# A delta-rule scan with a feed-forward block: writing the first four units' outputs together, one feature of w_out at a time

## The chip, the cores and the metric

The kernel runs on one core of a Trainium2 chip. The core has a matrix engine (TensorE, PE in the profile), a vector engine (DVE), an activation engine (ScalarE, ACT), a general engine (GpSimd, POOL), a sync engine (SP) that mostly issues transfers, and 16 DMA engines. Matrix products end in PSUM, which the kernel divides into eight banks of 128 partitions by 2 KB. The metric is the device time of one execution in microseconds (us), lower is better.

## The reference

A linear-attention scan by the delta rule, followed by a feed-forward block. For 4 batches, 8 heads, 768 positions and a head size of 48:

```python
k_n = k / (norm(k) + 1e-6)
state = 0                                   # (B, H, 48, 48)
for t in range(768):
    y[:, :, t] = einsum('bhd,bhde->bhe', q[:, :, t], state)
    v_old      = einsum('bhde,bhd->bhe', state, k_n[:, :, t])
    state     += beta_t * outer(k_n[:, :, t], v[:, :, t] - v_old)
x = y as (3072, 384)                        # heads side by side
h = x @ w_in                                # (384, 2048)
g = h * sigmoid(1.702 * h)
out = g @ w_out                             # (2048, 384)
```

q, k, v and beta are float32. w_in and w_out arrive as float64: two 32-bit words a number, which the kernel itself turns into float32.

## The kernel before

**Units.** The 768 positions are cut into 6 chunks of 128. A chunk of one batch is a unit, so there are 24, taken chunk by chunk: units 0 to 3 are the four batches of chunk 0. Two units make a half, whose 256 rows go through the feed-forward block together.

**The scan.** Inside a chunk the delta rule becomes a triangular system. Its 32x32 diagonal blocks are inverted on DVE (`invert`, two units at once from chunk 1 on, one step of the generator being a product and a reduction); the blocks of G go to DRAM and back to be laid out for it (Nd, NT), as does the result (Yd, XB). A unit is then solved in four blocks of 32 rows: `solve` (psU) multiplies by the inverse, ACT copies to US, `below` (psR) computes what the later rows lose, DVE subtracts it from V. `scores` makes psT, QS and psQ with the mask M (POOL selects the triangle). `queries` and `outputs` make psY, two tiles of a bank each, hold the new state in a part of one of them (psS), copy the unit's y to xT and add psS to the state ST. `woven` interleaves the steps of up to three units and, by `spend`, pieces of the feed-forward queue; its tuple STEPS says how many steps of the inversion stand at each of three places for odd and even n.

**The feed-forward block.** `hidden` computes ph = x @ w_in for two features of 128 at a time and writes gT = gelu(ph). `written` sums po = g @ w_out over 16 features for one unit. For the first half `both_written` (L771) does this for two units feature by feature, in the list `order` of features, since w_out is still being converted then; the second half follows with `written`. The queue is set up at L1108.

**Conversion.** Raw float64 words of w_out are fetched by `fetch_out` (L188) into buffers that are free at that time: parts of w_out itself (`inside`) or turns of the xT and M buffers (`outside`). The first eight of the order go by the queue of GpSimd, the others by that of SP. `conversions` yields the five DVE operations of a piece one after the other, with a Relu on ACT after the first of them; `fill(n)` takes n of these steps. When a piece is done, `fetches` starts the fetch that may use its place.

**Order.** The operations of each engine run in the order in which the program records them in this part (`pinned`, `sync`, `other_queue`, `beside`); each engine works down its own list, and waits where an operand isn't ready or a buffer is in use.

**PSUM.** Two banks are `ps_big` (psT, psG, half of psQ), four are `ps_seq` (psU, psR, psY, the other half of psQ), two are `ps_moe` (ph, po). A tile takes the next bank of its pool in turn and waits for the last reader of what was there.

Of the kernel before, what the change touches and what calls it, by code (L numbers as in the profile page):

```python
# [18 lines left out]
def kernel(  # L19
# [23 lines left out]
    C = 128  # L43
# [23 lines left out]
    io = ctx.enter_context(tc.tile_pool(name="io", bufs=3))  # L67
    wk = ctx.enter_context(tc.tile_pool(name="wk", bufs=2))
    ps_big = ctx.enter_context(tc.tile_pool(name="ps_big", bufs=2, space=PSUM))
    ps_seq = ctx.enter_context(tc.tile_pool(name="ps_seq", bufs=4, space=PSUM))  # L70
    ps_moe = ctx.enter_context(tc.tile_pool(name="ps_moe", bufs=2, space=PSUM))
    dram = ctx.enter_context(tc.tile_pool(name="dram", bufs=2, space=bass.MemoryType.DRAM))

# [26 lines left out]
    def pinned(op):  # L100

        return lambda *a, **kw: tc.keep_in_program_order(op(*a, **kw))  # L102

    class Engine:

# [75 lines left out]
                )  # L181

    places, slots = {}, {}
    inside = {3: 6, 4: 8, 5: 10, 6: 12, 7: 14, 12: 14, 13: 10}
    outside = {0: "xT", 8: "xT", 11: "xT", 1: "M", 9: "M", 14: "M", 2: "M2", 10: "M2", 15: "M2"}
    order = [0, 1, 2, 3, 4, 5, 6, 7, 8, 13, 9, 10, 12, 11, 14, 15]

    def fetch_out(f):  # L188

        if f in outside:  # L190
            slot = outside[f]
            if slot not in slots:
                slots[slot] = wk.tile([128, 2 * DM], I32, tag=slot[:2].strip("2"), name="raw", bufs=3)
            words = slots[slot]
        else:
            words = raws[:, inside[f] * DM : (inside[f] + 2) * DM]
        places[f] = as_raw(words, (1, DM))
        first = order.index(f) < FC // 2
        (other_queue if first else sync)(
            out=as_rows(places[f])[:, 0], in_=moe_w_out[f * 128 : (f + 1) * 128, :]  # L200
        )

# [50 lines left out]
    def conversions():  # L253

        whole = list(pieces())

        def begin(i):
            dst, raw, shape, name = whole[i]
            ops = conversion(dst, places[name[1]] if raw is None else raw, shape)
            next(ops)  # L260
            return ops

        after = begin(0)
        yield
        for i in range(len(whole)):
            ops = after
            next(ops)
            yield
            next(ops)
            yield  # L270
            if i + 1 < len(whole):
                after = begin(i + 1)
                yield
            next(ops)
            yield
            next(ops)
            done.add(whole[i][3])
            fetches.pop(whole[i][3], lambda: None)()
            yield
# [1 line left out]
    fetches = {  # L281
        ("in", 0, 1): lambda: fetch_in(3),
        ("in", 3, 1): lambda: fetch_out(3),
        ("out", 4): lambda: fetch_out(13),
        ("out", 6): lambda: fetch_out(12),
    }
    for new, old in ((8, 0), (9, 1), (10, 2), (11, 8), (14, 9), (15, 10)):
        fetches[("out", old)] = lambda f=new: fetch_out(f)
    converting = conversions()

# [266 lines left out]


    def bank(name, shape=(128, H, D)):
        return ps_seq.tile(list(shape), F32, tag="seq", name=name)  # L560

    lasts = [None]

    class Step:
# [19 lines left out]
        def scores(self):  # L584
# [7 lines left out]
            if c > 0:  # L592
# [1 line left out]
                act.activation(self.QS[:, :, S], St, ACT.Copy)  # L594
            yield
            self.M = (
                spare("M").rearrange("p (h t) -> p h t", h=H) if self.n in (B - 1, B + 1)
                else wk.tile([128, H, 128], F32, tag="M", name="M", bufs=3)
            )
            n = 128 + D if c > 0 else 128  # L600
            for g in range(0, NP, 2):
                pool_, tag = (ps_seq, "seq") if g else (ps_big, "big")
                ps = [pool_.tile([128, 2, 128 + D], F32, tag=tag, name="psQ") for _ in range(2)]
                for i in range(2):
                    for hh in range(2):
                        r = self.rows(hh)
                        pe.matmul(
                            ps[hh][:, i, 0:n], lhsT=self.kT[r, g + i, :],
                            rhs=self.QS[r, g + i, 0:n], start=True, stop=True,
                        )  # L610
                for hh in range(2):
                    hs = slice(2 * g + hh, 2 * g + 4, 2)
                    if c > 0:
                        Vh = self.V[:, hs, :]
                        vec.tensor_tensor(Vh, Vh, ps[hh][:, :, S], op=ALU.subtract)
                    copy = act.copy if hh == 0 or self.n < 2 * B + HB else vec.tensor_copy
                    copy(self.M[:, hs, :], ps[hh][:, :, 0:128])
                if g == 0:
                    yield
# [148 lines left out]
            nc.sync.dma_start(out=out[b * S + c * C : b * S + (c + 1) * C, :], in_=o)  # L768
            yield 1.3

    def both_written(c, gT):  # L771

        po = [ps_moe.tile([128, DM], F32, tag="moe", name="po") for _ in range(HB)]
        for n, f in enumerate(order):
            ahead = order[min(n + 3, FC - 1)]
            while ("out", ahead - ahead % 2 if 4 <= ahead < 8 else ahead) not in done:
                fill(1)
            for i in range(HB):
                pe.matmul(
                    po[i], lhsT=gT[f // FQ][:, f % FQ, i * C : (i + 1) * C], rhs=w_out[:, f, :],  # L780
                    start=(n == 0), stop=(n == FC - 1),
                )
            if n < FC - 1:
                yield 1.3
        for i in range(HB):
            o = wk.tile([128, DM], F32, tag="o", name="o")
            act.copy(o, po[i])
            sync(out=out[i * S + c * C : i * S + (c + 1) * C, :], in_=o)
        yield 1.3

    def take(cost):
# [73 lines left out]
            debt[0] -= done  # L865

    STEPS = (9, 5, 3, 3, 3, 3)
    begun = {}

    def woven(n, share):  # L870

# [3 lines left out]
        nonlocal inverting  # L875
        A, B_, D_ = steps.pop(n - 1, None), steps.get(n), steps.get(n + 1) or NoStep()
        m = n + B + 1
        if n < B + HB:
            K = normalize_mixed(m + 1) if n <= B else iter(())
        else:  # L880
            K = (normalize if n > 6 else normalize_mixed)(m) if m < len(units) else iter(())
# [2 lines left out]
            P = begun.pop(m)  # L884
        if n % HB == 1 and B < n and n + 1 + HB < len(units):
            inverting = invert(*units[n + 1 + HB], HB)
        ahead = STEPS[:3] if n % HB == 1 else STEPS[3:]

        next(K, None)
        together([(B_, 1)], [(A, 2)])  # L890
        run(D_.scored)
        next(K, None)
# [10 lines left out]
        together([(B_, 2)], [(D_, 0)])  # L903
        if A:
            A.queries()
            A.outputs()
        run(P)
        ahead_of(inverting, ahead[2])
        if n % HB == 0:
            run(inverting)  # L910
        spend(share / 6)
# [41 lines left out]
    late_U = room[:, 0 : H * D + XR]  # L953
    pool.memset(late_U[:, H * D :], 0.0)
    zs = room[:, 512 : 512 + 6 * B * H].rearrange("p (s b h) -> p s b h", s=6, b=B)
    psD = [ps_seq.tile([128, B, NP, BS], F32, tag="seq", name="psD") for _ in range(2)]
    warm(NW)
    for b in range(B):
        squares_first(b)
# [133 lines left out]
    load(B + 2, ((QP, q),), sync)  # L1093
    for n in range(2 * B + 1, 2 * B + 1 + HB):
        load(n, ((KN, k),), sync)
    for i in range(22):
        ahead_of(inverting, 1)
        if i < 18:
            feed()
        if i in (2, 3, 4, 7, 8, 9, 10):  # L1100
            fetch_out(i - 2 if i < 5 else i - 3)
    run(inverting)
    def beside_conversion(work):
        for cost in work:
            fill(2)
            yield cost

    queue = [beside_conversion(w) for w in ffn] + [both_written(0, gTs[0]), written(*units[HB], gTs[1])]  # L1108
    for n in range(B - 1, len(units) + 1):
        woven(n, 20.8 if n > 6 else 13.0)  # L1110
    run(take(1e9))
# [31 lines left out]
```

## Time and profile before

| | us |
|---|---|
| median of 3 runs | 771.1 |
| lowest and highest | 770.93, 772.66 |
| the profiled execution | 771.55 |
| its span | 769.8 |
| PE busy | 743.6 |
| DVE busy | 439.8 |
| ACT busy | 240.1 |
| POOL busy | 128.4 |
| first po begins | 135.13 |
| first ph of the third half | 215.10 |

The profile is of one execution. The span runs from its first to its last instruction, and lies 1.75 us under the execution's own time. Busy time is counted by engine. A row such as `po<-w_out,gT` names the tile that is written and the tiles read; a bracket at the end of a row of the timeline gives the idle time before it and the operation that ended it. The granted clock is the share of full speed at which TensorE was allowed to run. All recorded operations of the scan have one line, L102, so that rows are told apart by their tiles.

### The profile page before, as it was taken

The numbers are of one execution on the slowest core, as the hardware profiler recorded it, in microseconds if no ns is written. First come the engines' busy times: TensorE is split into PE (matmuls) and PEld (weight loads), VectorE is DVE, ScalarE is ACT, GpSimd is POOL, SyncE is SP. The second block draws the span as 40 slices with busy tenths as digits, with TensorE's granted clock in tenths as the row PEclk, the third lists the DMA queues.
The fourth block names the chain that finished last, engine by engine and source line by source line (L and its number), as shares of the span: only waits on it lengthen the run. The fifth ranks groups of instructions, "written<-read, shape, count | busy, mean of one in ns | idle before, by whom it ended". The sixth has DMA issues, their size and how long they took to land.

```text
span 769.8 us, 19471 instructions
## 1 busy us (share of the span) xinstructions
PE 743.6 (97%) x8508; PEld 558.0 (72%) x8508; DVE 439.8 (57%) x896; ACT 240.1 (31%) x535; POOL 128.4 (17%) x133
## 2 busy tenths in 40 slices
PE   7888999888999999999999999999999999999997
PEld 6666788556687687687688678678678677686774
DVE  5999897996766566566566566565566521000000
ACT  4567523343233233133133133124123132121110
POOL 6133301100222122122131121220210000000000
PEclk8599999989999999999999999999999999999999
DMA  9965355543142142142142142142030020000000
GB/s 158 173 121 114 86 146 124 141 107 82 40 96 57 37 93 56 37 95 56 35 96 57 34 97 56 25 107 57 22 81 9 24 42 2 17 11 1 26 1 21
DMA packets 131637, 50.78 MB, mean 66 GB/s; under 512 B 106432, under 2 KB 127040, under 8 KB 131552
## 3 DMA queue, kind: packets, MB, share of 16 engines
q1 hardware_dynamic: 129152, 41.27, 24.9%
q0 software_dynamic: 2400, 8.26, 4.4%
q8 instruction: 67, 1.10, 0.6%
q14 instruction: 18, 0.15, 0.1%
HBM read 32.08 MB, written 16.25 MB: 63 GB/s over the span
## 4 chain that ended last, share of the span: by engine, by line
PE 83%; DVE 8%; SPq 4%; issue 1%; ACT 1%; DMA 1%; POOL 0%; DVEq 0%; ACTq 0%
PE ph L102 32%; PE po L102 30%; PE psY L102 6%; PE psU L102 5%; SPq L102 4%; PE psQ L102 3%; PE psR L102 3%; PE psG L102 2%; DVE w_out L102 2%; PE psT L102 2%; DVE tmp L102 2%; DVE P L102 1%; DVE V L102 1%; DVE w_in L102 1%; DMA w_out<-in_moe_w_in_dram 1%
## 5 line engine op out<-in xcount | busy, mean ns | idle before, releaser
L102 PE MATMUL po<-w_out,gT 128*128 128x384 f32 x768 | 263.4, 494 | 3.3 <-DVE w_out L102 3.3
L102 PE MATMUL ph<-xT,w_in 128*128 128x256 f32 x1152 | 261.2, 383 | 0.3
L102 PEld LDWEIGHTS ph<-xT,w_in 128*128 128x128 f32 x1152 | 214.8, 190 | 32.5 <-issue 1.7
L102 PEld LDWEIGHTS po<-w_out,gT 128*128 128x128 f32 x768 | 142.2, 191 | 96.3 <-DVE w_out L102 4.2
L102 DVE TENSOR_TENSOR V<-V,psR 128x384 f32<-128x384 f32 (+2 forms) x72 | 40.1, 557 | 191.6 <-PE psR L102 191.0
L102 ACT ACTIVATE gT<-ph 128x512 f32<-128x512 f32 x96 | 56.5, 596 | 150.8 <-PE ph L102 150.7
L102 DVE TENSOR_TENSOR P<-NT,YB 64x8 f32<-64x8 f32 (+26 forms) x178 | 85.2, 479 | 4.7
L102 ACT COPY US<-psU 32x384 f32<-32x384 f32 x92 | 43.2, 470 | 139.6 <-PE psR L102 75.5
L102 PEld LDWEIGHTS psU<-V,XB 32*32 32x32 f32 x1536 | 58.3, 104 | 35.8 <-issue 25.6
L102 DVE TENSOR_REDUCE YB<-P 64x4 f32<-64x8 f32 (+27 forms) x178 | 77.2, 434 | 6.3 <-DVE P L102 0.2
L102 PE MATMUL psU<-V,XB 32*32 32x48 f32 x1536 | 69.5, 203 | 4.0 <-DVE V L102 3.9
L102 PE MATMUL psR<-US,G 32*32 32x48 f32 x2576 | 62.9, 204 | 1.0 <-issue 0.5
L624 POOL TENSOR_SCALAR_AFFINE_SELECT M<-M 128x1024 f32<-128x1024 f32 x20 | 25.1, 1253 | 220.9 <-DVE M L102 160.1
L102 PEld LDWEIGHTS psR<-US,G 32*32 32x32 f32 x2576 | 53.4, 104 | 2.0 <-issue 1.0
L102 PE MATMUL psQ<-QS,kT 48*128 48x176 f32 (+1 forms) x384 | 39.1, 350 | 5.4 <-ACT QS L102 5.4
L102 PEld LDWEIGHTS psQ<-QS,kT 48*128 48x128 f32 x384 | 32.1, 215 | 9.0 <-ACT QS L102 7.2
L102 DVE TENSOR_TENSOR P<-NT 64x256 f32<-64x256 f32 (+7 forms) x44 | 36.3, 825 | 0.3
L102 DVE TENSOR_REDUCE NT<-P 64x64 f32<-64x1024 f32 (+7 forms) x44 | 35.4, 803 | 1.5
L102 PE MATMUL psG<-kT 48*128 48x128 f32 x384 | 32.1, 304 | 1.9 <-ACT G L102 1.2
L102 ACT COPY o<-po 128x384 f32<-128x384 f32 x24 | 11.5, 479 | 71.5 <-issue 41.0
L87 POOL DMA_DIRECT2D KN<-in_k_dram x13 | 12.4, 953 | 116.1 <-PE psY L102 107.0
L102 ACT COPY M<-psQ 128x256 f32<-128x256 f32 x68 | 22.9, 377 | 24.8 <-DVE V L102 17.5
(102 smaller groups left out, 609.7 us busy)
## 6 DMA issues: line engine op xcount, KB each, us to landing
Nd<-G SPq DMA_DIRECT2D x16, 512.0 KB, 3.5
QP<-in_q_dram SPq DMA_DIRECT2D x24, 192.0 KB, 3.9
V<-in_v_dram SPq DMA_DIRECT2D x24, 192.0 KB, 3.3
out_dram<-o SPq DMA_DIRECT2D x24, 192.0 KB, 2.0
KN<-in_k_dram POOLq DMA_DIRECT2D x14, 192.0 KB, 3.8
NT<-Nd SPq DMA_DIRECT2D x20, 128.0 KB, 2.6
Yd<-YS SPq DMA_DIRECT2D x20, 128.0 KB, 2.5
XB<-Yd SPq DMA_DIRECT2D x20, 128.0 KB, 3.0
```

The source lines that it names most:

```text
L87: dma(out=dst[n % len(dst)][:, :, 0:D], in_=src[b, :, c * C : (c + 1) * C, :].rearrange("h p d -> p h d"),)
L102: return lambda *a, **kw: tc.keep_in_program_order(op(*a, **kw))
L624: (pool if self.n < B else nc.gpsimd).affine_select(out=self.M, in_=self.M, compare_op=ALU.is_gt, fill=0.0, base=0, pattern=[[0, H], [1, 1 ...
```

## The change

`both_written` for the first half and `written` for the second become `all_written` for both: four accumulators po, each feature of w_out serving four units. Two of them lie in `ps_moe`, two in one half of `ps_seq`, which is now two pools of two banks that are taken in turn (`seq`); while `all_written` is open (`turns[1]`), the scan has the other half alone. The four o copies follow one another at the end, two of them into a free gT buffer, and their transfers are issued by ScalarE (`beside`).

The order of features, the places of their raw words (now free gT buffers too) and what releases them are changed, and all raw words are fetched by GpSimd's queue; a conversion isn't begun before its fetch is recorded (`sent`). Steps of the conversion stand at other places: three with each two po matmuls, four instead of two beside `hidden` once w_in is done, five between a unit's output copies and its state's addition (`A.outputs(between)`), together with the steps of the inversion that stood behind. For n up to 6 the inversion's steps are divided by SOON instead of STEPS. The squares of one unit's keys are recorded earlier (`squared`), and one M moves from a gT buffer to the M buffers.

```diff
     io = ctx.enter_context(tc.tile_pool(name="io", bufs=3))
     wk = ctx.enter_context(tc.tile_pool(name="wk", bufs=2))
     ps_big = ctx.enter_context(tc.tile_pool(name="ps_big", bufs=2, space=PSUM))
-    ps_seq = ctx.enter_context(tc.tile_pool(name="ps_seq", bufs=4, space=PSUM))
+    ps_seq = [ctx.enter_context(tc.tile_pool(name=f"ps_seq{i}", bufs=2, space=PSUM)) for i in range(2)]
     ps_moe = ctx.enter_context(tc.tile_pool(name="ps_moe", bufs=2, space=PSUM))
     dram = ctx.enter_context(tc.tile_pool(name="dram", bufs=2, space=bass.MemoryType.DRAM))
 
...
     def pinned(op):
 
         return lambda *a, **kw: tc.keep_in_program_order(op(*a, **kw))
+
+    turns = [0, False]
+
+    def seq(shape, name):
+
+        if not turns[1]:
+            turns[0] ^= 1
+        return ps_seq[0 if turns[1] else turns[0]].tile(list(shape), F32, tag="seq", name=name)
 
     class Engine:
 
...
                 )
 
     places, slots = {}, {}
-    inside = {3: 6, 4: 8, 5: 10, 6: 12, 7: 14, 12: 14, 13: 10}
-    outside = {0: "xT", 8: "xT", 11: "xT", 1: "M", 9: "M", 14: "M", 2: "M2", 10: "M2", 15: "M2"}
-    order = [0, 1, 2, 3, 4, 5, 6, 7, 8, 13, 9, 10, 12, 11, 14, 15]
+    inside = {3: 6, 4: 8, 5: 10, 6: 12, 7: 14, 14: 10, 15: 12}
+    outside = {0: "xT", 8: "xT", 12: "xT", 10: "xT", 1: "M", 2: "M2", 9: "gT", 11: "gT", 13: "gT2"}
+    order = [0, 1, 2, 3, 4, 5, 6, 7, 8, 14, 15, 9, 12, 13, 10, 11]
 
     def fetch_out(f):
 
         if f in outside:
             slot = outside[f]
-            if slot not in slots:
+            if slot not in slots and slot[:2] == "gT":
+                slots[slot] = spare("raw").bitcast(I32)[:, 0 : 2 * DM]
+            elif slot not in slots:
                 slots[slot] = wk.tile([128, 2 * DM], I32, tag=slot[:2].strip("2"), name="raw", bufs=3)
             words = slots[slot]
         else:
             words = raws[:, inside[f] * DM : (inside[f] + 2) * DM]
         places[f] = as_raw(words, (1, DM))
-        first = order.index(f) < FC // 2
-        (other_queue if first else sync)(
+        other_queue(
             out=as_rows(places[f])[:, 0], in_=moe_w_out[f * 128 : (f + 1) * 128, :]
         )
 
...
 
         whole = list(pieces())
 
+        def sent(i):
+            return i >= len(whole) or whole[i][1] is not None or whole[i][3][1] in places
+
         def begin(i):
             dst, raw, shape, name = whole[i]
             ops = conversion(dst, places[name[1]] if raw is None else raw, shape)
...
             yield
             next(ops)
             yield
+            while not sent(i + 1):
+                yield
             if i + 1 < len(whole):
                 after = begin(i + 1)
                 yield
...
     fetches = {
         ("in", 0, 1): lambda: fetch_in(3),
         ("in", 3, 1): lambda: fetch_out(3),
-        ("out", 4): lambda: fetch_out(13),
-        ("out", 6): lambda: fetch_out(12),
+        ("out", 4): lambda: fetch_out(14),
     }
-    for new, old in ((8, 0), (9, 1), (10, 2), (11, 8), (14, 9), (15, 10)):
+    for new, old in ((8, 0), (15, 6), (12, 8), (10, 12), (11, 9)):
         fetches[("out", old)] = lambda f=new: fetch_out(f)
     converting = conversions()
 
...
 
 
     def bank(name, shape=(128, H, D)):
-        return ps_seq.tile(list(shape), F32, tag="seq", name=name)
+        return seq(shape, name)
 
     lasts = [None]
 
...
                 act.activation(self.QS[:, :, S], St, ACT.Copy)
             yield
             self.M = (
-                spare("M").rearrange("p (h t) -> p h t", h=H) if self.n in (B - 1, B + 1)
+                spare("M").rearrange("p (h t) -> p h t", h=H) if self.n == B - 1
                 else wk.tile([128, H, 128], F32, tag="M", name="M", bufs=3)
             )
             n = 128 + D if c > 0 else 128
             for g in range(0, NP, 2):
-                pool_, tag = (ps_seq, "seq") if g else (ps_big, "big")
-                ps = [pool_.tile([128, 2, 128 + D], F32, tag=tag, name="psQ") for _ in range(2)]
+                shape = [128, 2, 128 + D]
+                ps = [
+                    seq(shape, "psQ") if g else ps_big.tile(shape, F32, tag="big", name="psQ")
+                    for _ in range(2)
+                ]
                 for i in range(2):
                     for hh in range(2):
                         r = self.rows(hh)
...
             nc.sync.dma_start(out=out[b * S + c * C : b * S + (c + 1) * C, :], in_=o)
             yield 1.3
 
-    def both_written(c, gT):
-
-        po = [ps_moe.tile([128, DM], F32, tag="moe", name="po") for _ in range(HB)]
+    def all_written(c, gTs):
+
+        turns[1] = True
+        po = [
+            (ps_moe if i < HB else ps_seq[1]).tile([128, DM], F32, tag="moe" if i < HB else "seq", name="po")
+            for i in range(B)
+        ]
         for n, f in enumerate(order):
-            ahead = order[min(n + 3, FC - 1)]
+            ahead = order[min(n + 2, FC - 1)]
             while ("out", ahead - ahead % 2 if 4 <= ahead < 8 else ahead) not in done:
                 fill(1)
-            for i in range(HB):
+            for i in range(B):
                 pe.matmul(
-                    po[i], lhsT=gT[f // FQ][:, f % FQ, i * C : (i + 1) * C], rhs=w_out[:, f, :],
-                    start=(n == 0), stop=(n == FC - 1),
+                    po[i], lhsT=gTs[i // HB][f // FQ][:, f % FQ, i % HB * C : (i % HB + 1) * C],
+                    rhs=w_out[:, f, :], start=(n == 0), stop=(n == FC - 1),
                 )
-            if n < FC - 1:
-                yield 1.3
-        for i in range(HB):
-            o = wk.tile([128, DM], F32, tag="o", name="o")
+                if i % HB == HB - 1 and (n < FC - 1 or i < B - 1):
+                    fill(3)
+                    yield 1.3
+            if f == 3:
+                fetch_out(9)
+                fetch_out(13)
+        turns[1] = False
+        rest = spare("o")
+        for i in range(B):
+            o = wk.tile([128, DM], F32, tag="o", name="o") if i < HB else rest[:, i % HB * DM : (i % HB + 1) * DM]
             act.copy(o, po[i])
-            sync(out=out[i * S + c * C : i * S + (c + 1) * C, :], in_=o)
+            beside(out=out[i * S + c * C : i * S + (c + 1) * C, :], in_=o)
         yield 1.3
 
     def take(cost):
...
             debt[0] -= done
 
     STEPS = (9, 5, 3, 3, 3, 3)
-    begun = {}
+    SOON = (3, 6, 6, 4, 3, 3)
+    begun, squared = {}, {}
 
     def woven(n, share):
 
...
         nonlocal inverting
         A, B_, D_ = steps.pop(n - 1, None), steps.get(n), steps.get(n + 1) or NoStep()
         m = n + B + 1
-        if n < B + HB:
+        if m + 1 in squared:
+            K = squared.pop(m + 1)
+        elif n < B + HB:
             K = normalize_mixed(m + 1) if n <= B else iter(())
         else:
             K = (normalize if n > 6 else normalize_mixed)(m) if m < len(units) else iter(())
...
             P = begun.pop(m)
         if n % HB == 1 and B < n and n + 1 + HB < len(units):
             inverting = invert(*units[n + 1 + HB], HB)
-        ahead = STEPS[:3] if n % HB == 1 else STEPS[3:]
-
-        next(K, None)
+        ahead = SOON if n < B + HB + 1 else STEPS
+        ahead = ahead[:3] if n % HB == 1 else ahead[3:]
+
+        if n != B - 1:
+            next(K, None)
         together([(B_, 1)], [(A, 2)])
         run(D_.scored)
         next(K, None)
...
         together([(B_, 2)], [(D_, 0)])
         if A:
             A.queries()
-            A.outputs()
+            A.outputs((lambda: (fill(5), ahead_of(inverting, ahead[2]))) if n <= B + HB else None)
         run(P)
-        ahead_of(inverting, ahead[2])
+        if n > B + HB:
+            ahead_of(inverting, ahead[2])
         if n % HB == 0:
             run(inverting)
         spend(share / 6)
...
     late_U = room[:, 0 : H * D + XR]
     pool.memset(late_U[:, H * D :], 0.0)
     zs = room[:, 512 : 512 + 6 * B * H].rearrange("p (s b h) -> p s b h", s=6, b=B)
-    psD = [ps_seq.tile([128, B, NP, BS], F32, tag="seq", name="psD") for _ in range(2)]
+    psD = [seq((128, B, NP, BS), "psD") for _ in range(2)]
     warm(NW)
     for b in range(B):
         squares_first(b)
...
     load(B + 2, ((QP, q),), sync)
     for n in range(2 * B + 1, 2 * B + 1 + HB):
         load(n, ((KN, k),), sync)
+    squared[2 * B + 1] = normalize_mixed(2 * B + 1)
     for i in range(22):
         ahead_of(inverting, 1)
+        if i == 14:
+            next(squared[2 * B + 1])
         if i < 18:
             feed()
         if i in (2, 3, 4, 7, 8, 9, 10):
...
     run(inverting)
     def beside_conversion(work):
         for cost in work:
-            fill(2)
+            fill(4 if ("in", 3, 1) in done else 2)
             yield cost
 
-    queue = [beside_conversion(w) for w in ffn] + [both_written(0, gTs[0]), written(*units[HB], gTs[1])]
+    queue = [beside_conversion(w) for w in ffn] + [all_written(0, gTs)]
     for n in range(B - 1, len(units) + 1):
         woven(n, 20.8 if n > 6 else 13.0)
     run(take(1e9))
```

## The prediction

> **What bounds the kernel now.** I read the page first (sums, slices, chain), then the busy time by stretches of 10 us, then TensorE's waits, and last the rows of PE and DVE around the waits.
>
> ```profile
> span 769.8 us, 19471 instructions
> PE 743.6 (97%) x8508; PEld 558.0 (72%) x8508; DVE 439.8 (57%) x896; ACT 240.1 (31%) x535; POOL 128.4 (17%) x133
> PE   7888999888999999999999999999999999999997
> PEclk8599999989999999999999999999999999999999
> ```
>
> The kernel is bound by TensorE. Its idle time lies in the first slices (19.2 us each) and in the eighth to tenth. The change leaves all before 120 us as it was, so its room is the second place. By stretches (the columns are busy us and instructions of PE, weight loads, DVE, ACT and POOL, then the granted clock, the DMA share and GB/s):
>
> ```profile
> 130.00:140.00 10.00, 9.38 (x114) 6.57 (x112) 8.16 (x19) 4.95 (x9) 0.00 (x0) 1.00 0.70 190
> 140.00:150.00 10.00, 8.67 (x83) 5.57 (x84) 9.86 (x18) 3.76 (x9) 2.82 (x2) 1.00 0.56 123
> 150.00:160.00 10.00, 8.36 (x118) 5.13 (x116) 9.60 (x24) 4.36 (x9) 0.00 (x0) 1.00 0.33 96
> 160.00:170.00 10.00, 8.09 (x60) 5.58 (x61) 9.66 (x23) 4.75 (x12) 1.27 (x1) 0.72 0.68 162
> 170.00:180.00 10.00, 7.87 (x87) 4.54 (x86) 6.77 (x24) 2.07 (x5) 0.00 (x0) 0.94 0.19 52
> 180.00:190.00 10.00, 10.00 (x166) 7.13 (x165) 7.00 (x15) 2.72 (x7) 0.95 (x1) 1.00 0.30 79
> ```
>
> From 140 to 170 us DVE is the full engine, with the conversion of w_out's words (a piece of 384 takes 0.39+0.47+0.27+0.59+0.48 = 2.2 us from start to start, one of 768 3.8 us). PE waits for it, directly or through ACT, whose copies stand behind the Relu that every piece needs:
>
> ```profile
> PE po L102 <- DVE w_out L102: 3.3, 2, 2.1
> PE psQ L102 <- ACT QS L102: 2.6, 2, 1.8
> PE psT L102 <- ACT G L102: 1.1, 1, 1.1
> PE psG L102 <- ACT kT L102: 0.6, 1, 0.6
> ```
>
> The third loss is the clock, 0.72 above, seen best in stretches of 3.41 us:
>
> ```profile
> 157.55:160.96 3.41, 2.33 (x11) 1.32 (x10) 3.31 (x9) 2.17 (x4) 0.00 (x0) 1.00 0.70 214
> 160.96:164.38 3.42, 1.85 (x36) 1.03 (x34) 3.32 (x9) 1.74 (x4) 0.00 (x0) 1.00 0.89 221
> 164.38:167.79 3.41, 3.14 (x17) 2.75 (x18) 3.28 (x11) 1.72 (x5) 0.00 (x0) 0.50 0.45 76
> 167.79:171.20 3.41, 3.41 (x6) 1.70 (x6) 3.13 (x10) 0.79 (x3) 1.27 (x1) 0.50 0.41 84
> ```
>
> After a stretch with PE busy 1.85 of 3.42 us the clock is 0.50 for two stretches; after 2.33 it was not lowered. Half speed over 6.82 us, with PE busy 6.55, loses 3.3 us.
>
> **What there is to win.** The rows of PE, from the first po at 135.13 to the psU of 176.98:
>
> ```profile
> 135.13 1.76 PE L102 MATMUL po<-w_out,gT 128*128 128x384 f32 x4
> 164.65 2.72 PE L102 MATMUL psQ<-QS,kT 48*128 48x176 f32 x16 [1.85 <-ACT QS L102]
> 167.30 6.06 PE L102 MATMUL po<-w_out,gT 128*128 128x384 f32 x12
> 175.50 1.56 PE L102 MATMUL po<-w_out,gT 128*128 128x384 f32 x4 [2.13 <-DVE w_out L102]
> ```
>
> These 41.85 us hold 64 po rows of 0.335 us (5.36 for 16, from 141.57 to 146.93), three psT of 0.44, two psQ of 1.39, one psU of 0.79, three mixed psU and psR (0.85, 0.93, 0.86), one psG of 1.09: 30.1 us of work. So 11.7 us are waits and the low clock. PE's order of kinds and shapes is the same in the changed kernel, so the same 30.1 us stand there and at most 11.7 us can go.
>
> **The change part by part.** *Four units per feature.* A converted feature now serves four po matmuls, not two, so PE asks for features at half the rate. Feature 0 was converted at 130.56; with the earlier squares DVE no longer idles 2.52 us before the ssq of 122.79, so it is there by about 128. From there, by 2.2 and 3.8 us a piece and the scan's DVE work between, feature 4 is there at about 140 us and wanted at 150, feature 8 at 147 and wanted at 167 (eight po rows of 0.335 us a feature, with the scan between): the po waits (3.3 us) go. The pieces also end later, at about 177 us instead of 175.4, since DVE waits 2.3 us for NT and 2.6 us for raw words.
>
> *Fewer conversion steps at a time.* The copies of QS, kT and G on ACT are no longer behind a Relu that waits. Of these 4.3 us I keep 1.2: 0.7 at the first psQ (0.76 in before), 0.3 and 0.2 at later ones where US is copied. Gain of both with the clock: 11.7 - 1.2 = 10.5 us.
>
> *Banks.* While the four accumulators live, two lie in half of the scan's PSUM, and the scan has two banks of four. The row where this bites is the first psY, which took other banks at once:
>
> ```profile
> 183.19 0.67 PE L102 MATMUL psY<-QS,ST 48*64 48x128 f32 x16
> 183.32 0.55 DVE L102 TENSOR_TENSOR V<-V,psR 128x384 f32<-128x384 f32 x1 [0.39 <-PE psR L102]
> ```
>
> psY's two tiles now need the bank of psU and that of psR, the second free only when DVE has done V-psR. On DVE that subtraction stands behind the subtraction before (0.56), the inversion's first eight pairs (3.06 together, from 170.14 to 173.2) and the last 1.5 us of feature 11. The psR ends at about 173.2 and DVE is done at 177.4: a wait of 4.3 us. Lower end 0.6 (DVE not late: one subtraction of 0.56), upper end 6 (DVE later by 1.7, the difference between the POOL queue's landings of raw words, 4.0 and 5.7). I take 4.3, as the rows add up. The psU before it waits 0.55 for a bank likewise, the second psY 0.66.
>
> *Inversion steps 3, 6, 6.* For the first units fewer steps come early and more in the middle. The normalised KN of the next unit is then behind 6.95 us of inversion products (450, 1024, 768, 512 elements: 1.31+2.49+1.84+1.31) and psT waits about 1.8 for it; before there was no wait. Ends 0 and 3.5 (half of those products).
>
> *Outputs by ScalarE.* Four o copies (0.48) and four DMA issues now stand in ACT's order between QS and the next US. ACT issues none in this trace; SP's out_dram issues take 0.36, GpSimd's KN 0.95; I take 0.5, nearest to the former since it is the same transfer. The next psU needs the bank of the third accumulator, so behind QS two copies, two issues and the third copy: 0.48x3+0.5x2 = 2.4, of which 2.05 uncovered. The o buffers are shared with `last`, whose six xT DMAs (0.61 an issue) land about 6 us after the second psY; were they late, the second o copy would wait and the price be up to 5.1. SP's queue is freed of eight raw fetches and four outputs; nobody waited for it there.
>
> *Raw words by GpSimd.* Eight more issues of 0.6 us to 0.95 on POOL, in front of its selects (1.1 to 1.3) and pow. Landing 4.0 us where SP's took 3.1. The scan needs M of a select some 6 us later, so I put nothing on PE; if not covered, 0.9 for one issue. *State after a filling, squares earlier, M in its own buffers:* the ST add comes up to 3 us later, but QS<-ST is wanted 4 us after; the ssq of 0.55 only moves. Nothing, up to 0.5 if conversions and ST collide.
>
> **Sum.** -10.5 + 0.55 + 4.3 + 1.8 + 0.66 + 2.05 = -1.1 us at the first ph of the next half (215.10 in before); after that PE is full and the difference stays. A wait of 4.3 us leaves at least one 3.41 us stretch less than half filled, or two nearly so, and 1.85 was enough to lower the clock, so one lowering, 3.3 us: +2.2. The profiled execution took 771.55 (span 769.8 and 1.75 around it), so 773.75; it was 0.45 above the median of the runs, 771.1, and against that I predict 773.3.
>
> The Trainium skill ("TensorE: Matmul & The Clock Gate", Part 1, what's actually happening) has a window of 3413 ns that runs freely, and half speed after at least one idle window. The length agrees with the 3.41 us stretches here, but the window that lowered the clock was busy for 54%, not idle. By the page's rule a wait of 4.3 us holds a whole idle window in about one phase of four, and the likely sum would be the -1.1 without the 3.3; by the row it is +2.2. I go by the row.
>
> **The rivals.** *Even to slightly slower* (0.36): as summed, one lowering, 771 to 776. For it: all its terms are rows. *Faster* (0.28): DVE is not late at psY, because Nd and NT come back sooner (G's copy to NT was 7.3 us) or the raw words do. Then psY waits 1.0, psT 0.5, psU 1.0, and the clock holds: -10.5+0.55+1.0+0.5+0.66+1.0 = -6.8, so 764.3; half-way, 768. Against it: DVE needs the same 14 pieces plus the inversion. *Slower* (0.36): scarce banks and low clock feed each other. It decides as soon as a second of the three waits (psT, psU) empties a stretch to 54%: -1.1+6.6 = +5.5, 776.6; with the xT DMAs late (5.1 for 2.05), 779.7. For it: 1.8 and 2.05 us are each near the 1.57 idle that sufficed. *The change doesn't do what it says*, since raw words by POOL land too late and po still waits: each such wait adds 1 to 2 us, and I count it within the slower case.
>
> **How the numbers follow.** About 0.3% (2.3 us) is what a measurement of this kernel can tell from no change: 768.8 to 773.4. The middle case lies mostly within (0.28) and partly above (0.08); 0.02 of the others falls within. So faster 0.28, same 0.30, slower 0.42. Range: 766 to 780, leaving out the best of the faster case and a wait worse than all bounds; the middle case alone 771 to 776.
>
> **What would show it.** Right: no PE wait for w_out after 135 us; the row at 176.98 in before comes at about 167; PE waits for V at the first psY, for KN at a psT, for ACT's o copy at the psU after the last po; PEclk below 1 between 175 and 190. Wrong: psY starts at once, or the clock stays 1.00, and the time is below 768; or po still waits for w_out.

## The result

Measured beside five executions of the kernel before (median 771.59 us), the changed kernel took 776.38 us in the median of five (773.67 to 779.1), a ratio of 1.0061 with a 95% interval of 1.0034 to 1.0089. Its profiled execution took 776.38 us (span 774.7). Later, twelve executions of it beside 29 of the kernel before gave 775.08 against 773.65 us: 1.0017, interval 0.9994 to 1.004. So the change costs somewhere between nothing and 0.6%, and the kernel before itself lies anywhere from 770.7 to 777.3 us. A large part of both, though not all, goes back to one cause, a low clock early in the kernel (experiments 4 to 6).

First the waits of PE in the profile after, from 125 to 225 us (the columns are the tile that waited, what it waited for, us in total, how often, the longest):

```profile
PE psY L102 <- DVE V L102: 3.2, 1, 3.2
PE psU L102 <- DVE V L102: 2.0, 2, 1.2
PE psU L102 <- ACT o L102: 2.0, 1, 2.0
PE psT L102 <- DVE KN L102: 1.8, 1, 1.8
PE psY L102 <- ACT US L102: 1.0, 2, 0.5
PE psQ L102 <- ACT US L102: 0.5, 1, 0.5
PE psQ L102 <- ACT QS L102: 0.2, 1, 0.2
```

Of the list before nothing of size is left: no po waits for w_out, and QS, kT and G cost 0.2 us. In their place stand the waits that the prediction named: psY for V, psT for KN, psU for the copy of o. The rows of PE at the first psY:

```profile
137.12 1.76 PE L102 MATMUL po<-w_out,gT 128*128 128x384 f32 x4
...
177.73 0.43 PE L102 MATMUL psY<-QS,ST 48*64 48x128 f32 x2 [0.49 <-ACT US L102]
181.34 1.12 PE L102 MATMUL psY<-QS,ST 48*64 48x128 f32 x14 [3.18 <-DVE V L102]
...
217.51 0.23 PE L102 MATMUL psU<-V,XB 32*32 32x48 f32 x1 [1.98 <-ACT o L102]
...
219.70 5.66 PE L102 MATMUL ph<-xT,w_in 128*128 128x256 f32 x25
```

The first psY waits for the second of these two subtractions. Between them DVE works down six steps of the inversion (176.18 to 179.18) and three operations of the conversion (to 180.70):

```profile
175.60 0.56 DVE L102 TENSOR_TENSOR V<-V,psR 64x384 f32<-64x384 f32 x1
176.18 0.17 DVE L102 TENSOR_TENSOR P<-NT,YB 64x18 f32<-64x18 f32 x1
...
180.14 0.56 DVE L102 SCALAR_TENSOR_TENSOR w_out<-tmp,w_out 128x384 f32<-128x384 f32 x1
180.73 0.55 DVE L102 TENSOR_TENSOR V<-V,psR 128x384 f32<-128x384 f32 x1
```

And the clock around that wait, in stretches of 3.41 us (PE busy is the second figure, the granted clock stands ahead of the last two):

```profile
172.45:175.87 3.42, 3.03 (x13) 1.61 (x10) 3.29 (x9) 1.80 (x5) 0.00 (x0) 1.00 0.22 43
175.87:179.28 3.41, 1.37 (x82) 1.02 (x82) 3.00 (x14) 0.95 (x2) 0.00 (x0) 1.00 0.00 0
179.28:182.69 3.41, 1.35 (x18) 1.02 (x20) 3.21 (x9) 0.00 (x0) 0.00 (x0) 0.50 0.02 5
182.69:186.11 3.42, 3.42 (x40) 3.33 (x38) 3.21 (x7) 0.81 (x3) 0.60 (x1) 0.50 0.00 0
```

From the first po to the first ph of the third half the kernel now takes 82.58 us, and took 79.9 before (135.13 to 215.03; by its row that ph begins at 215.03, not at the 215.10 given above and used in the expectations). This stretch is used below to compare profiles. It explains 2.7 of the 4.9 us between the spans. Another 2.0 us lie ahead of it, where PE runs the same operations in both programs: the first po comes at 137.12 instead of 135.13. The page shows it in its second row of slices, the row of the clock (the before's reads 8599999989 in its first ten slices):

```profile
PE   7889999997889999999999999999999999999998
PEclk8586999998999999999999999999999999999999
```

The third and fourth slices (39 to 77 us) have a low clock that the profile before had not. By stretches, first of the kernel before and then of the changed one:

```profile
50.00:56.00 6.00, 3.90 (x127) 3.13 (x129) 5.55 (x11) 2.26 (x4) 2.85 (x3) 1.00 0.10 19
56.00:60.00 4.00, 3.47 (x81) 2.90 (x76) 3.87 (x7) 3.95 (x13) 1.02 (x2) 1.00 1.01 211
60.00:66.00 6.00, 4.87 (x77) 3.98 (x74) 5.80 (x11) 3.84 (x11) 4.00 (x3) 1.00 0.81 144
```

```profile
50.00:56.00 6.00, 4.82 (x118) 3.66 (x110) 5.77 (x11) 2.78 (x5) 2.80 (x2) 0.75 0.08 26
56.00:60.00 4.00, 4.00 (x49) 3.29 (x45) 3.87 (x7) 2.32 (x8) 1.12 (x1) 0.50 1.03 237
60.00:66.00 6.00, 6.00 (x67) 4.88 (x67) 4.72 (x9) 4.55 (x14) 3.07 (x3) 0.50 0.55 106
```

### The profile page after: what moved, and what is told of

The parts are those of the page before. It is cut to its first block, busy times and chain, and to the rows that moved or that the text cites. A ratio compares the mean times of both kernels' runs of the same rounds, so it can differ in the third digit from the quotient of the medians.

```text
span 774.7 us, 19464 instructions
## 1 busy us (share of the span) xinstructions
PE 749.7 (97%) x8508; PEld 565.0 (73%) x8508; DVE 436.3 (56%) x896; ACT 240.0 (31%) x535; POOL 132.9 (17%) x141
## 4 chain that ended last, share of the span: by engine, by line
PE 82%; DVE 11%; DMA 3%; issue 2%; ACT 1%; POOL 1%; DVEq 0%; POOLq 0%; ACTq 0%; SPq 0%
PE ph L102 30%; PE po L102 29%; PE psY L102 6%; PE psU L102 5%; PE psQ L102 3%; PE psG L102 3%; DVE P L102 3%; PE psR L102 3%; PE psT L102 2%; DVE YB L102 2%; DVE NT L102 2%; PE ps_warm L102 1%; DMA NT<-Nd 1%; DVE w_out L102 1%; DMA Nd<-G 1%
## 5 line engine op out<-in xcount | busy, mean ns | idle before, releaser
L102 PEld LDWEIGHTS psU<-V,XB 32*32 32x32 f32 x1536 | 60.2, 107 | 38.6 <-issue 28.3
L102 PE MATMUL psU<-V,XB 32*32 32x48 f32 x1536 | 71.2, 206 | 6.3 <-DVE V L102 4.0
L102 PE MATMUL psG<-kT 48*128 48x128 f32 x384 | 35.0, 325 | 1.2 <-ACT G L102 1.2
L102 PEld LDWEIGHTS psG<-kT 48*128 48x128 f32 x384 | 29.8, 223 | 3.7 <-ACT G L102 2.1
```

## The experiments

The theory: scarce banks make the first psY wait for DVE, this wait lowers the clock, and the keys and the o copies each add a wait of some 2 us. The rivals: the loss is the early low clock, which the change has no part in; or what is saved at one wait returns at another. All medians are of several executions beside those of the kernel before on the same chip, and a ratio is against these. Experiments 1 to 4 were measured together (before: 773.69 us, 770.76 to 776.82, 34 executions), so were 5 to 8 (773.65 us, 29 executions) and 9 to 11 (774.42 us, 11); 12 stands alone (773.43 us, 7). Each group ran on another chip, so that a difference in us between groups has the difference of the chips in it; the ratios are then the fairer figure.

**1. The inversion's steps behind the subtraction.**

```diff
-    SOON = (3, 6, 6, 4, 3, 3)
+    SOON = (3, 0, 12, 4, 3, 3)
```

> The inversion's steps of the first units are 3, 0, 12 instead of 3, 6, 6, so that the six that stood between the two subtractions of V on DVE (3.06 us) come behind the second. Measured by the stretch from the first po to the first ph of the third half: 79.97 us in the kernel before, 82.58 in the changed one. Theory (the scarce banks make the first psY wait for DVE, and that wait lowers the clock): psY's wait falls from 3.2 us to below 1.5, the clock stays at 1.00 after it, about 1 us of wait appears at the psR or psQ that need the state's addition, and the stretch is 77.5 to 79.5 us. Rival (the loss is the early lowering of the clock at 53 to 70 us, which has nothing to do with the change): the stretch may shrink, the time stays near 776 wherever the early lowering is there. Rival (the wait is on the bank as such, not on DVE's order): psY waits 2.5 us or more as before.

Median 770.84 us (768.5 to 774.22), ratio 0.9965 (0.9943 to 0.9986). The wait of the first psY for V fell to 0.27 us, a psR waits 0.65 for the state, the clock stays at 1.00 there, and the stretch is 78.8 us, although the clock is low for 3.41 us at another place in it, from 154.44:

```profile
175.42 0.66 PE L102 MATMUL psY<-QS,ST 48*64 48x128 f32 x14 [0.27 <-DVE V L102]
184.16 0.23 PE L102 MATMUL psR<-US,G 32*32 32x48 f32 x1 [0.65 <-DVE ST L102]
```

So the wait was DVE's order, not the bank alone. The median is 0.35% below the kernel before, where the changed kernel lies 0.17 to 0.6% above it.

**2. The order of the o copies.**

```diff
-        for i in range(B):
+        for i in (2, 3, 0, 1):
             o = ...
             act.copy(o, po[i])
```

> The o copies and their transfers are taken in the order of units 2, 3, 0, 1, so that the accumulator whose bank the next psU needs is copied first. Theory: the psU behind the last po waits 0.5 to 0.8 us instead of 1.98, and the stretch from the first po to the first ph of the third half is 1.2 to 1.5 us shorter than 82.58 us; if the late wait no longer matters to the clock, nothing else changes. Rival (the psU waits for the transfers on ScalarE's queue or for xT's transfers, not for the order of the copies): the wait stays at 1.5 to 2 us or is longer.

The wait of psU for o is gone from the list (0.5 to 0.8 us of it were expected to stay) and the stretch is 79.77 us, but the median is 775.13 us (772.11 to 779.68), ratio 1.0011 (0.999 to 1.0033), as the changed kernel alone. The profile shows a wait of psT for POOL's KN of 2.7 us at 227.97, where it was 0.9 and, in the second profile of the changed kernel (experiment 5), 1.2. The early clock blurs this comparison; it is made again in experiment 8.

**3. A bank more for psY.**

```diff
-            whole = [bank("psY", (128, 512)) for _ in range(2)]
+            whole = [bank("psY", (128, 512))]
+            if turns[1]:
+                whole.append(ps_big.tile([128, 512], F32, tag="big", name="psY"))
+            else:
+                whole.append(bank("psY", (128, 512)))
```

> While the four accumulators live, psY's second tile takes a bank of the pool of psT, psG and psQ instead of one of the scan's two. Theory (scarce banks): the 3.2 us wait of the first psY for V is gone; psG, which comes next and needs that bank, waits 0.5 to 1.2 us for the copies of psY; the clock isn't lowered between 175 and 190 us; the stretch from the first po to the first ph of the third half falls from 82.58 to 77 to 80 us. Rival (DVE is simply late, and what is late at psY is late at the next step anyway): the wait moves to the next psR or psQ and the stretch stays within 1 us of 82.6.

Median 772.49 us (767.2 to 774.83), ratio 0.9972 (0.995 to 0.9994). The first psY no longer waits for V, psG waits 0.2 us (expected 0.5 to 1.2), the clock isn't lowered, and the stretch is 76.89 us. The spread of 7.6 us goes with the mean clock: the seven executions at 0.967 to 0.971 took 771.97 us or more, the five at 0.976 to 0.982 took 771.61 or less.

```profile
173.44 0.67 PE L102 MATMUL psY<-QS,ST 48*64 48x128 f32 x16 [0.49 <-ACT US L102]
...
176.76 1.16 PE L102 MATMUL psG<-kT 48*128 48x128 f32 x14 [0.21 <-ACT xT L102]
```

**4. The early clock.**

```diff
-        warm(NU if i < 3 else NU // 2)
+        warm(NU)
```

> In the first stretch of the scan (40 to 60 us) the warming matmuls of the later steps are 11 instead of 5. Theory (the first po at 137.12 instead of 135.13 comes from the clock's lowering at 53 to 70 us, which happens in some executions by where a window of 3.41 us falls): with PE fuller there the lowering doesn't occur in any execution, the first po comes at 134.5 to 136 us, and the times lie closer together than 773.7 to 779.1, near 774. Rival (the first po is later for another reason, and the spread too): times and spread stay as they are, or grow where the warming matmuls are on the path.

Median 771.22 us, where I had expected about 774, all within 770.46 to 772.32, ratio 0.9965 (0.9947 to 0.9983). The first po comes at 133.79, and the clock holds where it was low:

```profile
50.00:56.00 6.00, 5.47 (x152) 4.53 (x143) 5.77 (x11) 2.82 (x6) 2.80 (x2) 1.00 0.07 25
56.00:60.00 4.00, 4.00 (x67) 3.45 (x68) 3.87 (x7) 3.90 (x14) 1.17 (x1) 1.00 1.02 238
```

The spread fell from 5.4 us to 1.9, which fits the early clock being its main part. The edit adds six matmuls of about 0.11 us (11 take 1.38 us, 5 take 0.72) in each of five steps in which PE waited anyway. In the stretch the waits of psY, o and KN are as they were (3.2, 2.0, 1.8), but it takes 79.45 us: no psU waits for V here, and the low clock behind the first psY lasts 3.41 us instead of 6.83.

**5. The changed kernel once more**, unaltered.

> The changed kernel as it is, measured beside 34 and more executions of the kernel before instead of 5. The kernel before lies at 770.8 to 772.8 us without and at 775.5 to 776.8 us with an early lowering of the clock (mean clock 0.966) here. Theory (both kernels draw the early lowering alike, and without it the changed one is about 2.6 us slower, which is the difference of their stretches from the first po to the first ph of the third half): median 775 to 777, the best 773, the ratio 1.002 to 1.005. Rival (the change is really slower by 0.6%): the ratio is 1.006 again. Rival (it is no slower, the first five executions of before were lucky): the ratio is within 0.001 of 1.

Median 775.08 (772.1 to 778.69) against 773.65 (770.66 to 777.31), ratio 1.0017 (0.9994 to 1.004). This profiled execution had no early low clock: first po at 134.11, stretch 81.82 us, 772.86 us in all. The three waits that were predicted are the same to 0.1 us (psY 3.18, o 1.99, KN 1.76); psU waits 1.3 us for V where it was 2.0. The program being the same, the 3.0 us between the two first po go with the early low clock. Of the 63 executions of the kernel before in these two sets (34 and 29), 28 have a mean clock of 0.966 or 0.967, as the first profile after had, and most of those lie at 775.5 us and above; that it is the early lowering in them too is inferred from the mean clock, not seen in their profiles. It doesn't explain all: at one mean clock, 0.977, 14 of the 63 lie at 770.7 to 772.2 and at 773.4 to 773.9 us, and no profile here says why. The first comparison had five executions of before, none above 772.7 us.

**6. The kernel before with the same warming**, the edit of experiment 4.

> The kernel before with the same 11 warming matmuls instead of 5 in the first stretch of the scan as the changed kernel had at 771.22 us. Theory (the early lowering is the same lottery in both): its times lie within 2 us of each other, the early lowering is in no execution, and the median is 768 to 770.5, that is 1 to 3 us below 771.22, since the stretch from the first po to the first ph of the third half is 79.97 us against 79.45 to 82.6. Rival (the two kernels are equal where the early clock is the same): 771 to 772.

Median 772.3 us (770.52 to 773.0), ratio 0.9971 (0.995 to 0.9992). Both kernels with warming are equal to within 0.15%, 771.22 and 772.3, so my theory's "1 to 3 us below" fell. So did "the early lowering is in no execution": this profile (772.82 us) has a low clock of 3.42 us from 73.28, and three more such in the stretch, where the first profile had 6.82 us in all. Its stretch is 81.46 us instead of 79.9, so the comparison of stretches, too, depends on where the clock happens to fall. Here po waits 3.7 us for w_out in one piece:

```profile
PE po L102 <- DVE w_out L102: 3.7, 1, 3.7
```

What the kernel before loses to conversion, the changed one loses to the banks, the keys and the o copies, with a low clock behind some of these waits.

**7. Warming and the bank together**, edits 3 and 4.

> The changed kernel with the warming matmuls and with psY's second tile in a bank of the pool of psT, psG and psQ. Theory (banks and the clock's lowering behind the first psY cost 4 to 6 us of which the extra bank showed 5.7 in the stretch): stretch 76.5 to 77.5 us against 79.45 with the warming alone, median 767 to 769. Rival (what is saved there is lost further on, at the keys that POOL normalises behind the inversion): median 770 to 771.5, with a wait of psT for KN at about 225 us.

Median 767.45 us (766.2 to 767.9), ratio 0.9916 (0.9891 to 0.9941), stretch 77.42 us. There is no wait for KN at 225 us. Against warming alone (771.22 us, ratio 0.9965) the bank is worth 3.8 us.

**8. Warming and the order of the o copies**, edits 2 and 4.

> The changed kernel with the warming matmuls and the o copies in the order of units 2, 3, 0, 1. Theory (the 1.4 to 2 us that the psU after the last po no longer waits come back as the wait of the next psT for the keys that POOL normalises, 2.7 us where it was 0.9, since that waits for NT by DRAM): no wait of the psU, a wait of 1.5 to 2.8 us at about 226 us, median within 0.7 us of 771.22. Rival (the gain was hidden by the early clock): median 769 to 770.

Median 771.28 us (769.79 to 772.86), ratio 0.9971 (0.9954 to 0.9988). The stretch is 1.4 us shorter than with warming alone (78.06 against 79.45), the time is the same. The profile's longest waits, up to 235 us:

```profile
PE psT L102 <- POOL KN L324: 3.3, 1, 3.3
PE psY L102 <- DVE V L102: 3.2, 1, 3.2
```

With warming alone the first of these lines is absent and there is 2.0 us for o. The low clock moves with the wait: 3.41 us of it stand behind psU's there, from 213 us, and behind this psT's here, from 228.13. On DVE the keys' rn stands behind NT (which is there at 219.79 after DVE idled 6.77 us for its transfer) and nine steps of the inversion:

```profile
219.79 1.22 DVE L102 TENSOR_TENSOR NT<-NT,bI 64x1024 f32<-64x1024 f32 x1 [6.77 <-DMA NT<-Nd]
224.91 0.56 DVE L102 TENSOR_TENSOR V<-V,psR 64x384 f32<-64x384 f32 x1
225.50 0.17 DVE L102 TENSOR_SCALAR rn<-rn 128x8 f32<-128x8 f32 x1
```

**9. The keys earlier**, edits 3 and 4 and:

```diff
-    SOON = (3, 6, 6, 4, 3, 3)
+    SOON = (3, 6, 6, 2, 4, 4)
```

> The changed kernel with warming, psY's extra bank, and the inversion's steps 3, 6, 6 and 2, 4, 4 instead of 3, 6, 6 and 4, 3, 3: the two products of 768 and 512 elements (3.15 us) now come behind the keys' normalisation on DVE. Theory (psT waits 1.8 us for the keys because of these steps): that wait falls below 0.4, the stretch from the first po to the first ph of the third half from 77.4 to about 75.8 us, the median from 767.45 to 765.5 to 766.5. Rival (DVE is full and the wait only moves): 1 to 2 us of wait for V or for the state's addition at the next psR or psY, median 767 to 768.

Median 766.26 us (765.84 to 767.78), ratio 0.99 (0.9878 to 0.9922); the wait fell from 1.77 to 0.27 us, the stretch from 77.42 to 75.16. Of its 2.3 us 1.2 reached the time. The profiles show why: in experiment 7 the low clock behind the o wait begins at 208.91, 2.1 us ahead of the stretch's end, here at 209.25, with 0.1 us of the stretch left, so that most of it is counted in one stretch and not in the other.

**10. The o copies and nine steps less in front of the keys**, edits 2, 3, 4 and:

```diff
-        ahead = SOON if n < B + HB + 1 else STEPS
+        ahead = SOON if n < B + HB + 2 else STEPS
```

> The changed kernel with warming, psY's extra bank, the o copies in the order of units 2, 3, 0, 1, and the steps 3, 6, 6 kept for one more unit (3 instead of 9 steps in front of the rn that POOL's keys need). Theory (without the wait for o the psT behind it waits for these keys, which stand on DVE behind nine steps of the inversion, 4 us from 222.0 to 225.9): neither wait is left, median 765 to 766 against 767.45. Rival (the keys wait for NT, which comes by DRAM, and not for the steps): psT still waits 1.5 us or more for KN at 220 to 228 us, median 767 to 768.

Median 763.92 us (763.5 to 764.43), ratio 0.9866 (0.9843 to 0.989), 3.5 us below experiment 7 and better than the 765 to 766 expected. psU no longer waits for o, the clock isn't lowered behind it, and psT waits 0.2 us for KN at 220.47. DVE idles 6.80 us for NT as in experiment 8 (6.77), but rn comes 2.6 us behind NT where it came 5.7 us behind. So it was the nine steps that held the keys; the wait for NT alone doesn't.

**11. All of it**, the edits of 2, 3, 4, 9 and 10.

> All of these together: warming, psY's extra bank, steps 2, 4, 4, o copies in the order 2, 3, 0, 1, and the steps 3, 6, 6 for one more unit. Theory (each wait of PE in this stretch is a term that adds): 767.45 - 1.7 - 1.7 = 764, within 763 to 765. Rival (what is saved runs into the next unit's round trip by DRAM): 765.5 to 767.5, with a wait for KN or for the inverse between 215 and 235 us.

Median 762.96 us (762.2 to 764.36), ratio 0.9856 (0.9832 to 0.988). The time is just under the 763 to 765 expected. The stretch is 73.18 us and the longest wait left in it 0.7 us:

```profile
PE psY L102 <- ACT US L102: 1.0, 2, 0.5
PE psR L102 <- DVE ST L102: 0.7, 1, 0.7
```

This version beats both kernels, by 1.4% the one before, of which 0.3% are the warming's (experiment 6).

**12. The outputs by SP**, edits 3 and 4 and:

```diff
-            beside(out=out[i * S + c * C : i * S + (c + 1) * C, :], in_=o)
+            sync(out=out[i * S + c * C : i * S + (c + 1) * C, :], in_=o)
```

> The changed kernel with warming and psY's extra bank, and the four outputs issued by SP instead of ScalarE, in their order 0, 1, 2, 3. Theory (two issues of 0.36 us each stand between QS and the third o copy): the psU behind the last po waits 1.2 to 1.4 us instead of 1.99, the rest being the two copies in front and the third itself; the median is 766.5 to 767.4 against 767.45. Rival (on SP the issues stand behind xT's six transfers, and the later copies of o behind nothing): the wait is 0.5 us or less. Rival (the issues cost ScalarE nothing): it stays at 1.9 to 2.0 us.

Median 764.86 us (764.49 to 765.15), ratio 0.9886 (0.9863 to 0.9908), 2.6 us below experiment 7 (by the ratios 0.3%, 2.3 us), where I had expected 0 to 1. The wait for o fell from 1.99 to 0.82 us, and ScalarE goes on to US and M sooner. ScalarE's rows, first of experiment 7, then of this one:

```profile
205.33 0.47 ACT L102 COPY o<-po 128x384 f32<-128x384 f32 x1
205.83 0.38 ACTq L102 DMA_DIRECT2D out_dram<-o  x1
206.41 0.48 ACT L102 COPY o<-po 128x384 f32<-128x384 f32 x1 [0.61 <-ACT o L102]
...
208.60 0.48 ACT L102 COPY o<-po 128x384 f32<-128x384 f32 x1 [0.82 <-ACT o L102]
...
209.49 0.47 ACT L102 COPY US<-psU 32x384 f32<-32x384 f32 x1 [0.41 <-ACT o L102]
```

```profile
205.44 1.66 ACT L102 COPY o<-po 128x384 f32<-128x384 f32 x4
207.67 0.47 ACT L102 COPY US<-psU 32x384 f32<-32x384 f32 x1 [0.57 <-PE psR L102]
```

Four copies take 1.66 us without issues and 3.75 us with them. The next US ends 1.8 us sooner; on SP nothing waits for the outputs, which leave behind xT's transfers.

As far as these two profiles show, the earlier US and M are not what the 2.6 us are made of, since PE waits for neither in either profile: from 200 to 300 us its waits are those for o and 0.2 us at a psG. The clock makes the difference. In experiment 7 the stretch with the o wait and the one behind it are:

```profile
205.50:208.91 3.41, 1.42 (x38) 1.02 (x38) 0.14 (x1) 1.57 (x4) 0.00 (x0) 1.00 0.97 254
208.91:212.33 3.42, 3.42 (x19) 2.86 (x18) 1.72 (x6) 1.93 (x6) 0.13 (x1) 0.50 1.17 296
```

Half speed over 3.42 us with PE busy throughout loses 1.7 us; in the profile of this experiment the clock isn't lowered there. The shorter wait (1.2) and the clock (1.7) together make 2.9 us, and the two profiled executions differ by 2.7.

## Why the prediction was right, and where not

The forecast was 773.3 us, 2.2 above the kernel before. The two measurements of that difference are 4.8 and 1.4 us, so the forecast lies between them; 776.38 is within the range. By its own steps:

- *What there is to win.* Predicted 10.5 us by the psU at 176.98 in before, 41.85 us behind the first po. It comes 33.0 us behind in the first profile after, 32.35 in the second and 31.24 with warming: a gain of 8.9 to 10.6. With warming it is the 10.5 predicted. In the other two it is short by two waits that I had not counted at that place: a psU for V (1.19 and 0.58 us) and a psQ for US (0.53 and 0.52).
- *The first psY.* Predicted 4.3 us: 3.18, and 0.49 for US ahead of it. Its two causes, the bank and DVE's order, are shown by undoing either (experiments 1 and 3). The psU before it, predicted 0.55, waited 0.82 and 0.72 us in the two profiles.
- *The clock behind it.* Predicted one lowering, 3.3 us. All five profiled executions with the 3.2 us wait (the two of the changed kernel, experiments 2, 4 and 8) have one that begins between 173 and 180 us, and none of the seven without the wait does. In the first it lasted 6.83 us, with PE busy 1.35 and 3.42: 2.4 us lost, less than predicted since part of it fell on the wait itself.
- *Steps 3, 6, 6.* Predicted 1.8: measured 1.75, and experiment 9 takes it away. The prediction has no wait there in the kernel before; there was one, 0.37 us at 201.15, so the step's price is 1.4.
- *Outputs by ScalarE.* Predicted 2.05 us of wait: 1.98. But the term has no clock in it: where the clock is lowered behind this wait, as in experiment 7, 1.7 us come on top, and experiment 12, which shortens the wait by 1.2 us, gains 2.6.
- *Second psY.* Predicted 0.66 for V: 0.49 for US.
- *Sum.* -1.1 and 3.3, so +2.2: the stretch grew by 2.7 in the first profile and 1.9 in the second. The measured terms, with the keys at 1.4, add up to 1.9 and 1.1, so 0.8 us stand in no term. That the forecast came so near is in part luck: it had the gain up to 1.7 us too large, and psY and the clock too dear by 0.6 and 0.9.
- *A second lowering,* which the slower case rested on, did not come from psT's 1.8 us. After the wait for o one came in some profiled executions (experiments 1, 4, 7 and 9: beginning between 208 and 214 us, 3.4 us long) and not in others (experiment 3, the changed kernel twice).
- *After that PE is full and the difference stays.* This sentence failed: at 232 us a psT waits 0.9 us for POOL's keys (1.2 at 229 us in the second profile), and 2.7 to 3.3 us as soon as an earlier wait is gone (experiments 2 and 8).
- *Not foreseen:* the early low clock, about 3 us between the two profiles of the changed kernel. "All before 120 us as it was" holds of PE's work, not of its time. It is the likely reason why the same pair of kernels lay 0.6% apart in one comparison and 0.2% in the other: the five executions of before in the first were all among the faster ones.

The page of the Trainium skill ("TensorE: Matmul & The Clock Gate", Part 1) would have made the sum -1.1, since the window in question wasn't idle. The profile after decides for the row: the window with PE busy 1.37 of 3.41 us lowered the clock. But my reading of the row, a bound near 54%, does not hold either, as the last section shows.

## What to carry to other kernels

When accumulators are doubled, list which tiles then share the banks that are left, and follow who must release each: here the wait for one subtraction on a full engine, with the low clock behind it, took back some 5 to 6 us (the stretch without it, experiment 3, is 4.9 and 5.7 us shorter than the changed kernel's two) of the 8.9 to 10.6 that the change had won. Count the issue of a transfer as work of the engine that issues it, and count the clock with each wait of the matrix engine that it makes longer. And before two kernels are compared at half a per cent, look in their profiles for a place early in both where the clock falls in some executions, and try to fill it.

## What the runs showed of the hardware

The share of PE's busy time in a stretch of 3.41 us does not tell whether the clock is lowered. In the second profile of the changed kernel a stretch with PE busy 1.65 of 3.41 us was followed by full clock (first fence); in experiment 1 one with 2.36 of 3.41 us was followed by half (second fence), and in experiment 6 even one with 2.91 (third fence):

```profile
195.90:199.31 3.41, 1.65 (x13) 0.77 (x6) 3.24 (x8) 0.94 (x2) 0.00 (x0) 1.00 0.29 58
199.31:202.73 3.42, 3.42 (x49) 2.08 (x50) 2.70 (x6) 0.60 (x1) 0.00 (x0) 1.00 0.00 0
```

```profile
151.03:154.44 3.41, 2.36 (x97) 2.10 (x98) 3.25 (x9) 1.34 (x3) 0.00 (x0) 1.00 0.39 121
154.44:157.85 3.41, 3.41 (x7) 1.82 (x6) 3.27 (x9) 2.64 (x5) 0.00 (x0) 0.50 0.04 10
```

```profile
69.87:73.28 3.41, 2.91 (x96) 2.34 (x95) 3.02 (x6) 2.62 (x7) 0.00 (x0) 1.00 0.74 142
73.28:76.70 3.42, 3.42 (x91) 2.63 (x91) 2.35 (x5) 1.57 (x3) 0.00 (x0) 0.50 0.12 28
```

The first stretch is by time almost only po (128x128 by 384), the second and the third hold 80 psU and psR (32x32 by 48) each, beside others. That the size of the matmuls counts and not the time they take fits this, but no run here tried it by itself. The issue of an output's transfer took ScalarE 0.34 to 0.43 us for the first two of four, and 0.34 to 1.13 us for the third and the fourth.
